# The last batch's queries turned by two DMA transposes instead of sixteen TensorE transposes, with the list of steps remade

## The chip, the cores and the metric

The kernel runs on one core of one Trainium2 chip. A core has five engines that run beside each other: TensorE (PE: matmuls, and transposes done as matmuls against an identity), VectorE (DVE), ScalarE (ACT), GpSimd (POOL) and SyncE (SP, which here only issues DMAs), and sixteen DMA engines that move data between HBM and the core's SBUF. The metric is device time in microseconds (us), the median over several executions. A profile of one further execution records every instruction; its span, from the first to the last instruction, is a little shorter than the time of the same execution.

## The reference

Efficient attention over 8 batches of 8 heads, 576 tokens and 64 elements a head, followed by a highway layer of width 512 over the 4608 tokens.

```
q_s = softmax(q, axis=-1)            # over the 64 elements of a head
k_s = softmax(k, axis=2)             # over the 576 tokens
kv  = einsum('bhsd,bhse->bhde', k_s, v)
x   = einsum('bhsd,bhde->bhse', q_s, kv)   # heads side by side: 4608 x 512
H   = maximum(x @ w_h, 0)
T   = sigmoid(x @ w_t + b_t)
out = T * H + (1 - T) * x            # float32, 4608 x 512
```

All inputs and the output are float32; the kernel works in fp16 inside.

## The kernel before

**Tiles.** The 4608 rows are worked in 36 tiles of 128 rows. Two batches make nine tiles: four of the even batch, four of the odd one, and one that holds half of each. Tiles 27 to 30 belong to batch 6, tiles 31 to 34 to batch 7, and tile 35 to both. Tiles 0, 4 and 5 are worked in two halves.

**Steps of a batch.** `k`, `v` and `q` (L180, L192) load it, 1152 KB of each. In batches 4 to 7 (`WIDE`, L186) a row of the landed query is one whole token with all its heads: two loads of 512 KB (L198) bring the tokens of the four whole tiles, and a third of 128 KB (L202) those of the shared tile. `ek` (L249) and `eq` (L293) are exponentials on ACT; `vc` (L255) casts V to fp16 on POOL, ACT or DVE, two calls a batch; `kv` (L261) multiplies K and V in 72 small matmuls; `kr`, `kn` (L277, L282) normalise the product on DVE. `qt` (L307) turns the exponential of the query on PE, so that the head's elements lie on the partitions: groups 0 and 1 are eight 128x128 transposes each for two tiles, group 2 is two transposes for the shared tile. The result is in PSUM, and `qc` (L326) copies it to SBUF on DVE or ACT.

**Steps of a tile.** `xu` (L337) multiplies the turned query, which it asks of `turned_q` (L334), by the batch's KV: four matmuls, whose last columns are the softmax's sums. `rs` and `x` (L356, L361) divide by them on DVE. `xt` (L368) turns x in four PE transposes, `xe` (L375) copies that to SBUF on DVE or ACT. `bw` (L382) puts the bias in PSUM, on PE, or on ACT if its step is marked `:A`; `mt` and `mh` (L394, L402) are the two products of four 512-wide matmuls each; `th` (L416) is a tanh on ACT. `dd` (L425), `uu` (L435), `ee` (L429) and `oo` (L451) combine them: in most tiles `dd` and `uu` run on DVE and `oo` on POOL; in a tile whose `uu` is marked `:P` ("lifted", L411), `uu`, `ee` and `oo` all run on POOL. `st` (L462) stores, from SP or, marked `:A`, from ACT's queue.

**What sets the order.** `ORDER` (L16 to L62) is a list of steps written out in advance; a step names its function, its batch or tile and a part, and after a colon an engine. The program is recorded in that order, so every engine executes its own steps in the order of the list and waits where an input or a buffer is not ready. Loads and nearly all stores go through SP's one queue: an SP instruction that waits holds up those behind it. `fill` (L165) steps are matmuls on zeros whose result nobody reads.

**Buffers.** The pools at L86 to L101 rotate: three landing tiles for each of k, q and v, four turned-query tiles, three each for `dd`, `uu`, `ee` and `th`, seven pairs of output tiles, two PSUM banks each for the two products, one for turned queries.

Of the kernel before, what the change touches and what calls it, by code (L numbers as in the profile page):

```python
# [9 lines left out]
FP16 = mybir.dt.float16  # L10
# [3 lines left out]


ORDER = """  # L16
b_0 b_32 k_0_1 v_0_1 k_0_3 setuppool k_0_0 setupdve vc_0_1 fill_16 q_0_0 ek_0_0 ek_0_3 v_0_2 eq_0_0 v_0_0 ek_0_1 fill_16
fill_12 vc_0_2:A bsplit k_0_2 vc_0_0:A v_0_3 q_0_4 vc_0_3:D fill_6 ek_0_2 bp eq_0_1 w_h_0 qt_0_0 fill_4 w_h_2 w_t_0
whd_1:P kv_0_0 whd_3:P fill_9 qc_0_0 kv_0_1 kr_0_0 fill_12 w_t_2 qt_0_1 fill_2 bc kr_0_1 kn_0_1 kn_0_0 xu_1_0 whd_0
rs_1_0 qc_0_1:A x_1_0 whd_2:P xu_0_1 rs_0_1 fill_12 fill_2 x_0_1 xu_0_0 whc_2 eq_0_2 xu_3_0 q_1_0 whc_0:A fill_9 rs_3_0  # L20
xt_1_0 wtc_2:P k_1_2 v_1_2 eq_1_0 wtc_0:P bw_1 qt_0_2 x_3_0 rs_0_0 xe_1_0:D ek_1_2 xt_3_0 xe_3_0:D xu_2_0 rs_2_0 x_0_0
vc_1_3 x_2_0 bw_3 mh_1_0 mh_3_0 xt_0_0 xt_0_1 xe_0_0 mt_3_0 mt_1_0 dd_1 ek_1_3 qc_0_2 v_1_0 th_3_0 qt_1_0 vc_1_2:A
xe_0_1:D mh_0_1 th_1_0 dd_3 k_1_0 uu_3_0 q_1_4 uu_1_0 q_2_0 kv_1_1 kr_1_1 qc_1_0:A xt_2_0 mh_0_0 xe_2_0 kn_1_1 bw_2
vc_1_0 bw_0 mt_0_1 dd_0 xu_5_1 ek_1_1 ek_1_0 mt_2_0 xu_4_1 rs_5_1 x_5_1 rs_4_1 vc_1_1 kv_1_0 x_4_1 eq_1_1 mt_0_0 xt_5_1
kr_1_0 th_2_0 eq_1_2 qt_1_1 k_2_0 xe_5_1 bw_5 kn_1_0 qc_1_1 v_2_0 xu_5_0 th_0_0 mt_5_1 rs_5_0 q_3_0 k_3_0 x_5_0 qt_1_2
ee_0 xu_4_0 bw_4 xt_5_0 xe_5_0:D xu_6_0 rs_4_0 rs_6_0 mh_2_0 x_4_0 xt_4_1 oo_1_0 uu_0_0:P xt_4_0 x_6_0 qc_1_2:A oo_0_0
mt_5_0 xu_8_0 eq_2_2 dd_2 mh_5_0 eq_2_0 fill_0 mh_5_1 xe_4_0:D xe_4_1 rs_8_0 eq_2_1 x_8_0 xt_6_0 dd_5 th_5_0 qt_2_0
xu_7_0 ek_2_2 oo_3_0 uu_2_0:P ee_2 mt_4_1 xe_6_0:D mt_4_0 qc_2_0 rs_7_0 ek_2_0 x_7_0 v_3_0 mh_4_1 vc_2_0:A xt_8_0 mh_4_0
uu_5_0 mh_6_0 qt_2_1 vc_2_2 xe_8_0:D kv_2_0 bw_6:A dd_4 th_4_0 mh_8_0 dd_6 q_4_0 kr_2_0 uu_4_0:P oo_2_0 kn_2_0 bw_8:A
qc_2_1:A eq_3_0 mt_6_0 xu_9_0 xt_7_0 dd_8 rs_9_0 mt_8_0 qt_2_2 x_9_0 xu_10_0 th_6_0 xe_7_0 k_4_0 xt_9_0 uu_6_0 oo_5_0  # L30
mh_7_0 th_8_0 rs_10_0 q_4_9 bw_7:A qc_2_2 x_10_0 ee_4 qt_3_0 xu_12_0 xe_9_0 oo_4_0 eq_3_2 uu_8_0 mt_7_0 oo_6_0 vc_3_0
ek_3_0 rs_12_0 bw_10:A th_7_0 eq_3_1 xt_10_0 mh_9_0 dd_7 x_12_0 vc_3_2 xe_10_0:D xu_11_0 qc_3_0 v_4_0 oo_8_0 xt_12_0
rs_11_0 x_11_0 uu_7_0 mh_10_0 xe_12_0:D mt_10_0 ek_3_2 v_5_0 bw_9 kv_3_0 k_5_0 q_5_0 th_10_0 bw_12:A eq_4_0 dd_10 mt_9_0
dd_9 uu_10_0:P kr_3_0 th_9_0 xt_11_0 qt_3_1 st_1_1:A kn_3_0 xu_14_0 mt_12_0 xe_11_0:D rs_14_0 mh_12_0 x_14_0 ee_10
uu_9_0 oo_7_0 xu_13_0 xt_14_0 dd_12 eq_4_1 oo_10_0 mh_11_0 oo_9_0 th_12_0 rs_13_0 xe_14_0:D bw_11:A v_6_0 qc_3_1:A
x_13_0 mt_11_0 uu_12_0 xu_15_0 ek_4_0 xt_13_0 bw_14:A mh_14_0 rs_15_0 xe_13_0 x_15_0 dd_11 qt_3_2 xu_16_0 oo_12_0
mt_14_0 ek_4_2 xt_15_0 qc_3_2 th_11_0 rs_16_0 th_14_0 vc_4_2 ee_11 dd_14 bw_13:A vc_4_0:A x_16_0 st_1_0 mh_13_0
xe_15_0:D uu_11_0:P xu_17_0 uu_14_0 rs_17_0 x_17_0 vc_5_2 bw_16:A xt_16_0 qt_4_0 xe_16_0 dd_13 qc_4_0 mt_13_0 kv_4_0
kr_4_0 qt_4_1 th_13_0 eq_4_2 oo_11_0 kn_4_0 xt_17_0 mh_15_0 q_5_9 qc_4_1 bw_15:A xu_18_0 k_6_0 mt_16_0 ek_5_2 qt_4_2
vc_5_0 rs_18_0 ek_5_0 st_3_0 ee_13 eq_5_1 dd_15 uu_13_0:P eq_5_0 ee_15 th_16_0 bw_17:A x_18_0 mh_16_0 oo_14_0 kv_5_0  # L40
xe_17_0:D dd_16 xt_18_0 qc_4_2 mt_15_0 th_15_0 ee_16 qt_5_1 kr_5_0 kn_5_0 oo_13_0 xe_18_0:D xu_20_0 qc_5_1 bw_18:A
rs_20_0 q_6_0 q_7_0 mh_17_0 mt_17_0 x_20_0 vc_6_2:A uu_15_0:P th_17_0 xu_21_0 qt_5_0 st_3_1 dd_17 rs_21_0 x_21_0 mt_18_0
xt_21_0 mh_18_0 oo_15_0 qc_5_0 vc_6_0:A xe_21_0:D xt_20_0 uu_16_0:P st_5_0 eq_5_2 oo_16_0 xu_19_0 st_5_1 th_18_0 uu_17_0
rs_19_0 xe_20_0:D bw_20:A mh_21_0 bw_21:A x_19_0 mt_20_0 xu_22_0 dd_21 dd_18 ek_6_2 ee_18 st_7_1 uu_18_0:P oo_17_0
rs_22_0 xt_19_0 ek_6_0 x_22_0 xe_19_0:D mt_21_0 mh_20_0 th_21_0 st_7_0 k_7_0 th_20_0 bw_22:A kv_6_0 xt_22_0 dd_20 qt_5_2
uu_21_0 eq_6_1 bw_19:A mh_19_0 kr_6_0 xe_22_0:D eq_6_0 kn_6_0 v_7_0 uu_20_0:P ee_20 st_10_1 mt_22_0 oo_18_0 dd_19
oo_20_0 q_7_9 xu_23_0 rs_23_0 qc_5_2 mh_22_0 x_23_0 th_22_0 qt_6_0 oo_21_0 xt_23_0 xu_24_0 mt_19_0 dd_22 eq_7_1 xe_23_0
mh_23_0 rs_24_0 qc_6_0 eq_7_0 bw_23:A x_24_0 xu_25_0 rs_25_0 xt_24_0 ee_22 x_25_0 th_19_0 qt_7_0 xe_24_0:D qc_7_0:A
uu_19_0 st_14_1 oo_19_0 mt_23_0 xu_26_0 rs_26_0 th_23_0 xt_25_0 qt_6_1 x_26_0 mh_24_0 bw_24:A xu_27_0 dd_23 uu_22_0:P
xe_25_0 mt_24_0 oo_22_0 qc_6_1:A ek_7_0 rs_27_0 xt_26_0 st_10_0 xe_26_0 x_27_0 th_24_0 qt_7_1 xu_29_0 uu_23_0 dd_24  # L50
rs_29_0 st_8_0 mh_25_0 x_29_0 bw_25:A oo_23_0 ek_7_2 vc_7_2 mh_26_0 uu_24_0 bw_26:A xu_28_0 rs_28_0 xt_29_0 xe_29_0
mt_25_0 q_6_9 th_25_0 x_28_0 qc_7_1:A dd_25 st_16_1:A vc_7_0 dd_26 oo_24_0 uu_25_0 mt_26_0 xt_27_0 th_26_0 bw_27:A
kv_7_0 bw_29:A xe_27_0:D mh_29_0 uu_26_0:P kr_7_0 mh_27_0 xt_28_0 st_12_1:A st_12_0 st_16_0:A kn_7_0 dd_29 xu_31_0
eq_6_2 mt_27_0 rs_31_0 x_31_0 ee_26 oo_25_0 xe_28_0 st_14_0 dd_27 mt_29_0 oo_26_0 xu_30_0 rs_30_0 xt_31_0 qt_6_2 th_27_0
mh_28_0 bw_28:A mt_28_0 th_29_0 xe_31_0:D x_30_0 st_21_0 uu_27_0:P st_19_0 xu_33_0 uu_29_0 eq_7_2 mh_31_0 xt_30_0 qc_6_2
rs_33_0 st_17_0:A bw_31:A th_28_0 xe_30_0 st_26_0 x_33_0 qt_7_2 dd_28 ee_27 dd_31 mt_31_0 st_25_0 oo_27_0 xu_32_0
oo_29_0 uu_28_0 xt_33_0 th_31_0 mh_30_0 xe_33_0 rs_32_0 x_32_0 st_23_0 bw_33:A mh_33_0 xu_34_0 uu_31_0 dd_33 mt_33_0
rs_34_0 xt_32_0 qc_7_2 bw_30:A x_34_0 xe_32_0:D dd_30 mt_30_0 xu_35_0 xt_34_0 th_33_0 oo_28_0 bw_32:A rs_35_0 th_30_0
uu_30_0 xe_34_0 bw_34:A mh_32_0 x_35_0 dd_32 ee_33 mt_32_0 oo_31_0 mt_34_0 st_31_0 xt_35_0 uu_33_0:P oo_33_0 mh_34_0
th_32_0 uu_32_0 st_28_0 oo_30_0 bw_35_1 xe_35_0 mt_35_1 st_33_0 th_34_0 dd_34 bw_35_0:A th_35_1 st_30_0 uu_34_0 oo_32_0  # L60
oo_34_0 mh_35_0 st_32_0:A mt_35_0 st_34_0 dd_35 uu_35_1 th_35_0 uu_35_0 oo_35_0 oo_35_1:D st_35_1:A st_35_0
# [4 lines left out]
def kernel(  # L66
# [10 lines left out]
    nc = tc.nc  # L77
    B, H, S, D = q.shape
    DM = H * D
    P = 128  # L80
    NP = 64
# [9 lines left out]
    eqp = pool("eqp", 4)  # L91
# [25 lines left out]
    T = {}  # L117

    def once(name, make):
        if name not in T:  # L120
            T[name] = make()
        return T[name]
# [57 lines left out]
    def load_kv(which):  # L180
        def step(e, b, c):
            n = (1, 2)[b] if b < 2 else 4
            nc.sync.dma_start(landing(which, b)[:, c:c + n], rows_of(which, b)[:, c:c + n])  # L183
        return step

    WIDE = (4, 5, 6, 7)  # L186
    MAIN = 4 * 2 * 4 * D
# [274 lines left out]
    def st(e, i, h):  # L462
# [60 lines left out]
```

## Time and profile before

| | us |
|---|---|
| time, median of 3 runs (lowest, highest) | 122.44 (122.19, 122.52) |
| time of the profiled execution | 122.46 |
| its span | 120.6 |
| PE busy | 110.4 (92%), of it 100 fills 13.4 |
| DVE busy | 94.0 (78%) |
| ACT busy | 95.1 (79%) |
| POOL busy | 88.5 (73%), 90 instructions |
| PE transposes of a query, 8 in a group (L316) | start to start 0.45 for the eight |
| ACT copy of a turned group (L330) | 1.01 to 1.04 |

The profile's timeline gives an instruction's start and its length; the start of the next one on the same engine tells how fast they really follow each other, which is less than the length where instructions overlap in a pipeline. A bracket behind a row tells how long the engine was idle before it and what ended the wait. The granted TensorE clock is full (0.998).

The DMA engines moved 40.08 MB in the span, a mean of 332 GB/s.

### The profile page before, as it was taken

Reading aid. Unit: us, or ns where it says so; the run is one execution under the profiler, and the core shown is the slowest. Engines: PE = TensorE matmul, PEld = TensorE weight load, DVE = VectorE, ACT = ScalarE, POOL = GpSimd, SP = SyncE. Lnnn points to the kernel's source line nnn. Section 1 sums busy time; section 2 is a strip of 40 time slices with the busy share of each in tenths; the row PEclk is TensorE's granted clock in tenths of the full one; section 3 lists DMA queues with packets and bytes.
Section 4 is the critical chain, followed back from the end, with each engine's and each line's share of the span. In section 5 each row is a group of like instructions: output and inputs, shape, how many; then the busy total and the mean of one; then the engine's idle time right before and its main releaser. Section 6 shows DMA issues by size and latency. Waiting matters only on the chain.

```text
span 120.6 us, 3576 instructions
## 1 busy us (share of the span) xinstructions
PE 110.4 (92%) x1426; PEld 69.2 (57%) x1426; DVE 94.0 (78%) x226; ACT 95.1 (79%) x146; POOL 88.5 (73%) x90
## 2 busy tenths in 40 slices
PE   5984999989899999999999999999999999999920
PEld 4863897454555656565657565556566655654510
DVE  5600877589599889989998998989789988999570
ACT  4049565798859999899999899999999966758710
POOL 5300043356597499999899999799999799969960
PEclk9999999999999999999999999999999999999999
DMA  3999999999999999999999999999999989910865
GB/s 105 296 359 387 382 379 377 391 374 387 390 386 393 391 387 358 379 361 394 396 373 365 380 389 355 358 377 376 382 366 293 280 201 353 353 42 23 325 261 174
DMA packets 22628, 40.08 MB, mean 332 GB/s; under 512 B 3282, under 2 KB 9682, under 8 KB 22612
## 3 DMA queue, kind: packets, MB, share of 16 engines
q1 hardware_dynamic: 21856, 38.15, 89.1%
q10 hardware_dynamic: 756, 1.71, 4.7%
q8 instruction: 11, 0.18, 0.6%
q14 instruction: 5, 0.04, 0.1%
HBM read 30.41 MB, written 9.44 MB: 331 GB/s over the span
## 4 chain that ended last, share of the span: by engine, by line
PE 60%; DMA 17%; ACT 9%; SPq 6%; issue 2%; DVE 2%; POOLq 1%; DVEq 0%; ACTq 0%
PE tps L399 21%; PE gps L407 20%; DMA q<-in_q_dram 17%; SPq L183 6%; PE turned L372 6%; PE xu L350 5%; PE qps L316 3%; PE kv L268 3%; ACT qe L297 2%; ACT ek L252 2%; PE qps L321 1%; ACT tps L423 1%; ACT tps L387 1%; ACT v L258 1%; ACT th L421 1%
## 5 line engine op out<-in xcount | busy, mean ns | idle before, releaser
L399 PE MATMUL tps<-w16t,xT 128*128 128x512 f16 (+1 forms) x148 | 36.8, 373 | 0.1
L407 PE MATMUL gps<-w16h,xT 128*128 128x512 f16 x144 | 36.5, 379 | 0.0
L365 DVE TENSOR_TENSOR x<-xu,rs 128x512 f16<-128x512 f32 (+1 forms) x39 | 25.0, 646 | 1.7
L460 POOL TENSOR_TENSOR o<-u,x 128x512 f32<-128x512 f16 (+1 forms) x22 | 24.9, 1136 | 1.7 <-DVE u L442 1.3
L427 DVE SCALAR_TENSOR_TENSOR d<-x,gps 128x512 f16<-128x512 f16 x36 | 24.0, 679 | 1.5 <-PE gps L407 1.1
L252 ACT ACTIVATE ek<-k 128x1152 f16<-128x1152 f32 (+1 forms) x20 | 18.9, 971 | 5.2 <-DMA k<-in_k_dram 5.2
L399 PEld LDWEIGHTS <-xT 128*128 128x128 f16 x148 | 13.4, 98 | 11.6 <-DVE xT L379 0.5
L440 POOL TENSOR_TENSOR u<-th,d 128x512 f16<-128x512 f16 x14 | 16.2, 1156 | 4.2 <-DVE rz L280 2.5
L407 PEld LDWEIGHTS <-xT 128*128 128x128 f16 x144 | 12.8, 98 | 10.6 <-ACT xT L379 0.3
L387 ACT COPY tps<-ball 128x512 f32<-128x512 f32 (+1 forms) x29 | 16.8, 586 | 2.1 <-DVE u L442 1.9
L433 POOL TENSOR_TENSOR e<-d,x 128x512 f16<-128x512 f16 x14 | 16.2, 1155 | 2.7 <-DVE d L427 2.7
L258 POOL CAST v<-v 128x1152 f16<-128x1152 f32 (+1 forms) x12 | 12.2, 1029 | 6.2 <-DMA v<-in_v_dram 6.2
L460 POOL TENSOR_TENSOR o<-u,e 128x512 f32<-128x512 f16 x14 | 16.1, 1155 | 0.5
L442 DVE SCALAR_TENSOR_TENSOR u<-tps,d 128x512 f16<-128x512 f32 (+1 forms) x23 | 15.1, 661 | 1.7 <-ACT tps L423 1.5
L167 PE MATMUL turned<-blank 128*128 128x256 f16 x100 | 13.4, 292 | 1.3 <-POOL blank L149 1.3
L350 PE MATMUL xu<-kvb,eq 128*128 128x130 f16 (+1 forms) x160 | 14.6, 224 | 0.0
L372 PE MATMUL turned<-idh,x 128*128 128x128 f16 x144 | 14.1, 219 | 0.4 <-ACT xT L379 0.3
L423 ACT ACTIVATE tps<-tps 128x512 f32<-128x512 f32 (+1 forms) x23 | 13.0, 566 | 1.7 <-PE tps L399 1.7
L350 PEld LDWEIGHTS <-eq 128*128 128x128 f16 (+1 forms) x160 | 10.5, 100 | 5.9 <-DVE x L365 1.5
L372 PEld LDWEIGHTS <-x 128*128 128x128 f16 x144 | 10.1, 98 | 5.1 <-issue 0.7
L297 ACT ACTIVATE qe<-q 128x1024 f16<-128x1024 f32 (+1 forms) x12 | 10.0, 843 | 3.9 <-DMA q<-in_q_dram 3.9
L167 PEld LDWEIGHTS <-blank 128*128 128x128 f16 x100 | 10.1, 105 | 3.0 <-POOL blank L149 1.3
(49 smaller groups left out, 127.7 us busy)
## 6 DMA issues: line engine op xcount, KB each, us to landing
k<-in_k_dram SPq DMA_DIRECT2D x6, 1152.0 KB, 12.8
v<-in_v_dram SPq DMA_DIRECT2D x6, 1152.0 KB, 12.4
q<-in_q_dram SPq DMA_DIRECT2D x10, 512.0 KB, 12.2
out_dram<-o SPq DMA_DIRECT2D x17, 256.0 KB, 5.6
out_dram<-o SPq DMA_DIRECT2D x6, 512.0 KB, 3.9
q<-in_q_dram SPq DMA_DIRECT2D x2, 1152.0 KB, 15.5
out_dram<-o ACTq DMA_DIRECT2D x6, 256.0 KB, 2.6
q<-in_q_dram SPq DMA_DIRECT2D x2, 640.0 KB, 10.3
```

Source lines behind the costliest of these rows:

```text
L167: nc.tensor.matmul(spare, blank[:, 0:P], blank[:, 0:2 * P], start=True, stop=True, skip_group_check=True)
L252: nc.scalar.activation(t[:, :, c:c + n].rearrange("p j c d -> p c j d"), T[f"k32{b}"][:, c:c + n].rearrange("p c (j d) -> p c j d", j=NJ), ...
L350: nc.tensor.matmul(dst, turned_q(b, jp, n), kvb[b % NKV][:, hh, kk], start=True, stop=True, skip_group_check=True)
L365: nc.vector.tensor_mul(t[:, k0:k1], sums(i, k)[:, :, :, 0:64], T[f"rs{i}_{k}"][:, 0:k1 - k0].unsqueeze(3).to_broadcast([P, k1 - k0, 4, D]))
L372: nc.tensor.matmul(t[:, n], T[f"x{i}"][:, n * P:(n + 1) * P], idh, is_transpose=True, start=True, stop=True, skip_group_check=True)
L387: nc.scalar.copy(t[:, cs], ball[:, cs])
L399: nc.tensor.matmul(T[gate(i, k)][:, cs], T[f"xT{i}"][:, n], w16["t"][:, n, cs], start=False, stop=(n == parts[-1] and not first), skip_gro ...
L407: nc.tensor.matmul(t, T[f"xT{i}"][:, n], w16["h"][:, n], start=(first and n == parts[0]), stop=(n == parts[-1] and not (first and len(part ...
L427: nc.vector.scalar_tensor_tensor(t, T[f"x{i}"], -0.5, T[f"gps{i}"], op0=ALU.mult, op1=ALU.max)
L433: eng.tensor_add(T[f"e{i}"], T[f"d{i}"], T[f"x{i}"])
L440: eng.tensor_mul(t, T[f"th{i}"], T[f"d{i}"])
L460: eng.tensor_add(t[:, cs], T[f"u{i}"][:, cs], T[f"{'e' if lifted(i) else 'x'}{i}"][:, cs])
```

## The change

The sixteen PE transposes of batch 7's two groups (`qt_7_0`, `qt_7_1`) and their two copies (`qc_7_0`, `qc_7_1`, both on ACT) are gone. In their place a new step `dt` issues, from SP, one DMA transpose for each group: it reads 128 rows of 1024 fp16 elements (256 KB) from the exponential in SBUF and writes eight turned 128x128 blocks to a new tile `eqd` in SBUF. `turned_q` takes batch 7's whole tiles from there. Group 2 of batch 7, and all other batches, are turned on PE as before.

```diff
+    def dt(e, b, g):
+        t = once(f"eqd{b}", lambda: eqp.tile([P, 4, 2, 2, NP * 2], FP16, tag="eqd", bufs=1, name=f"eqd_{b}"))
+        eng = nc.scalar if e == "A" else nc.sync
+        main = T[f"qe{b}"].rearrange("p j c d -> p (j c d)")[:, MAIN // 2 * g:MAIN // 2 * (g + 1)]
+        eng.dma_start(t[:, 2 * g:2 * g + 2].rearrange("p j h k t -> p (j h k) t"), main, transpose=True)
+
     def turned_q(b, jp, n):
+        if f"eqd{b}" in T and jp < 4:
+            return T[f"eqd{b}"][:, jp, n % 2, n // 2]
         return T[f"eq{b}_{jp // 2}"][:, jp % 2, n]
```

The whole list of steps is new. Its first lines, the lines with batch 7's query and KV, and its end:

```diff
 ORDER = """
-b_0 b_32 k_0_1 v_0_1 k_0_3 setuppool k_0_0 setupdve vc_0_1 fill_16 q_0_0 ek_0_0 ek_0_3 v_0_2 eq_0_0 v_0_0 ek_0_1 fill_16
-fill_12 vc_0_2:A bsplit k_0_2 vc_0_0:A v_0_3 q_0_4 vc_0_3:D fill_6 ek_0_2 bp eq_0_1 w_h_0 qt_0_0 fill_4 w_h_2 w_t_0
+b_0 b_32 k_0_0 k_0_1 k_0_3 q_0_0 setuppool k_0_2 ek_0_0 ek_0_1 v_0_3 ek_0_2 v_0_1 setupdve v_0_0 bsplit fill_12 fill_12
+fill_9 eq_0_0 fill_16 fill_16 qt_0_0 vc_0_0:A q_0_4 v_0_2 eq_0_1 vc_0_1:D fill_12 w_t_0 vc_0_3 w_t_2 qc_0_0 kv_0_0
...
-rs_22_0 xt_19_0 ek_6_0 x_22_0 xe_19_0:D mt_21_0 mh_20_0 th_21_0 st_7_0 k_7_0 th_20_0 bw_22:A kv_6_0 xt_22_0 dd_20 qt_5_2
...
-mh_23_0 rs_24_0 qc_6_0 eq_7_0 bw_23:A x_24_0 xu_25_0 rs_25_0 xt_24_0 ee_22 x_25_0 th_19_0 qt_7_0 xe_24_0:D qc_7_0:A
...
-xe_25_0 mt_24_0 oo_22_0 qc_6_1:A ek_7_0 rs_27_0 xt_26_0 st_10_0 xe_26_0 x_27_0 th_24_0 qt_7_1 xu_29_0 uu_23_0 dd_24
...
-mt_25_0 q_6_9 th_25_0 x_28_0 qc_7_1:A dd_25 st_16_1:A vc_7_0 dd_26 oo_24_0 uu_25_0 mt_26_0 xt_27_0 th_26_0 bw_27:A
-kv_7_0 bw_29:A xe_27_0:D mh_29_0 uu_26_0:P kr_7_0 mh_27_0 xt_28_0 st_12_1:A st_12_0 st_16_0:A kn_7_0 dd_29 xu_31_0
...
+xe_23_0 k_7_0 th_22_0 mt_23_0 xt_24_0 uu_22_0 mh_23_0 rs_25_0 eq_6_2 x_25_0 eq_7_1 th_23_0 eq_7_0 xe_24_0:D xu_26_0
+uu_19_0:P bw_24:A mh_24_0 dd_23 st_10_0:A st_10_1 ee_19 rs_26_0 xt_25_0 uu_23_0 mt_24_0 xe_25_0 dt_7_0 oo_19_0 x_26_0
+xu_27_0 qc_6_1 th_24_0 st_14_0 dd_24 bw_25:A oo_22_0 mh_25_0 ee_24 rs_27_0 xt_26_0 mt_25_0 bw_26:A vc_7_2:A x_27_0
+xu_29_0 xe_26_0:D oo_23_0 xt_27_0 vc_7_0 qt_6_2 th_25_0 q_7_9 ek_7_2 dd_25 dt_7_1 rs_29_0 mt_26_0 ek_7_0 x_29_0 uu_25_0
+xu_28_0 mh_26_0 bw_27:A st_17_0 xe_27_0:D mh_27_0 st_14_1 uu_24_0:P rs_28_0 x_28_0 qc_6_2 st_12_0 oo_24_0 xt_29_0
+st_12_1 th_26_0 kv_7_0 oo_25_0 dd_27 st_23_0 dd_26 uu_26_0:P kr_7_0 mt_27_0 xe_29_0 bw_29:A xt_28_0 mt_29_0 th_27_0
+st_16_1 kn_7_0 xu_31_0 ee_26 mh_29_0 xe_28_0 st_25_0 rs_31_0 uu_27_0 x_31_0 oo_26_0 th_29_0 bw_28:A eq_7_2 dd_29 mh_28_0
+uu_29_0:P ee_29 xu_30_0 oo_27_0 rs_30_0 xt_31_0 x_30_0 xe_31_0 mt_28_0 st_26_0 th_28_0 bw_31:A dd_28 qt_7_2 bw_30:A
+st_8_0:A xt_30_0 xe_30_0:D xu_33_0 rs_33_0 mh_31_0 x_33_0 mt_31_0 dd_31 xt_33_0 th_31_0 xe_33_0 xu_32_0 rs_32_0 mt_30_0
...
-th_32_0 uu_32_0 st_28_0 oo_30_0 bw_35_1 xe_35_0 mt_35_1 st_33_0 th_34_0 dd_34 bw_35_0:A th_35_1 st_30_0 uu_34_0 oo_32_0
-oo_34_0 mh_35_0 st_32_0:A mt_35_0 st_34_0 dd_35 uu_35_1 th_35_0 uu_35_0 oo_35_0 oo_35_1:D st_35_1:A st_35_0
+xe_34_0 xt_35_0 bw_34:A dd_32 st_21_0 xe_35_0:D oo_33_0 th_32_0 st_16_0 oo_30_0 mh_34_0 st_19_0 uu_32_0 mt_34_0 st_28_0
+st_31_0 oo_32_0 bw_35_1 mh_35_0 st_33_0 fill_0 dd_34 th_34_0 mt_35_1 bw_35_0:A mt_35_0 uu_34_0 dd_35 th_35_1 th_35_0
+uu_35_1 st_30_0 fill_16 st_32_0 uu_35_0 oo_34_0 st_34_0 oo_35_0:D st_35_0 oo_35_1:D st_35_1:A
 """
```

Counted over the two lists: fills 100 before and 109 after; `bw` on PE 8 and 6, on ACT 29 and 31; lifted tiles 14 and 17, and `uu` on DVE 23 and 20; `xe` on ACT 17 and 20, on DVE 22 and 19; `qc` on ACT 8 and 5, on DVE 16 and 17; casts of `w_t` on POOL 2 and 1, on ACT none and 1; subtractions of the identity (`whd`) on POOL 3 and 4; `oo` on POOL 36 and 35. The weights `w_t` are loaded ahead of `w_h` instead of behind. Batches 0 and 1 and the weights are still loaded first, up to the last part of batch 1's query (`q_1_4`), then `q_2`, `k_2`, `v_2`; of the last batch `v_7` is now loaded ahead of `k_7`.

## The prediction

> **What bounds the kernel now.** I read the page's forty slices first (3.0 us each), to see who is full where.
>
> ```profile
> PE   5984999989899999999999999999999999999920
> POOL 5300043356597499999899999799999799969960
> DMA  3999999999999999999999999999999989910865
> ```
>
> PE is full almost to its end, but its first seven digits are partly `fill`. POOL is nearly as full from the middle on, and the DMA engines are full up to slice 32. So three things are close to binding, and each stage has to be looked at. Next I read the timelines of the opening, and the waits' last releasers.
>
> ```profile
> 20.55 1.89 PE L407 MATMUL gps<-w16h,xT 128*128 128x512 f16 x8
> ...
> 29.32 1.06 ACT L297 ACTIVATE qe<-q 128x1024 f16<-128x1024 f32 x1 [0.51 <-DMA q<-in_q_dram]
> ...
> 30.43 0.62 PE L321 MATMUL qps<-idh,qe 128*128 128x128 f16 x8 [0.44 <-ACT qe L297]
> ...
> 38.43 1.15 POOL L258 CAST v<-v 128x1152 f16<-128x1152 f32 x1 [0.70 <-DMA v<-in_v_dram]
> ```
>
> Up to 30.4 us the loads set the pace: `q_1_4` lands at 29.3, its exponential ends at 30.3, and `qt_1_1` starts on PE at 30.43. `v_2` lands at 38.4, and `kv_2` starts at 40.14. From there PE hardly stops: what its starts lose to 115.45 comes to some 2.5 us in small pieces, half of it around `kv`'s small matmuls, the longest 0.42. The chain of waits says the same: from 44.68 on it is PE alone, until the last matmul. These are two of its lines and its end:
>
> ```profile
> 50.74 0.21 PE tps L389
> ...
> 82.98 0.45 PE qps L316 x8
> ...
> 115.00 0.45 PE tps L399 x4
> 115.45 0.02 issue
> 115.48 0.38 ACT tps L423
> ```
>
> The bound is PE's work from 30.43 on, and then a tail of 5.1 us (120.6 - 115.45).
>
> **The opening.** Both lists load the same bytes ahead of `q_1_4`, so I take 29.3 for its landing again. The other half of the argument is whether PE has done as much by then. Before, it has done `mt` 0 to 3, `mh` 0, 1, 3, both halves of `kv_0` and `kv_1`, and the two halves of `xu` that need `qt_1_0`. In the new list, `w_t` comes where `w_h` came (15.2 and 16.6), so `mt_3` can start near 19.0, ahead of 20.55; `w_h` comes where `w_t` came (18.3 and 20.0), POOL subtracts the identity until 21.4 and ACT's two `whc` (1.0 each) end at 23.3, so `mh` is 2.8 us later than before. Both fit in front of `qt_1_1`: the same steps are done by 30.4, and one more half of `xu` (0.12). What hides the later `mh` is the wait for `q_1_4`; beyond 30.4 it would cost one for one. Then `kv_2` could start at 39.4 by the sum of PE's steps and waits for `v_2` to about 40.1, as before.
>
> **PE's sum from `qt_1_1`.** By the start-to-start times of the rows (0.86 for each `mt` or `mh`, 0.23 for `xu`, 0.22 for `xt`, 0.21 for `bw`, 0.45 for eight `qt`):
> - `qt_7_0` and `qt_7_1`: 2 x 0.45 = -0.90.
> - `bw_4` and `bw_9` go to ACT: 2 x 0.21 = -0.42.
> - the half `xu` done earlier: -0.12.
>
> -1.44 in all. The stage from 84 to 95 us where the transposes stood is one in which PE is full, so they were on the path. With the old stalls and pieces kept (0.8 of them the wait for `v_2`) PE ends at 115.45 - 1.44 = 114.0.
>
> **ACT and DVE.** Over the list ACT loses three `qc` of 0.9 and gains two `bw` (0.52), three `xe` (0.5) and one cast of 1.0: +0.8, most of it before 40 us. From `kv_2` on, ACT has 66 us of work and DVE 68 beside PE's 73.4. Their changes are taken at nothing; PE's work covers them.
>
> **POOL.** This one isn't free. Three more lifted tiles are six operations of 1.115 (start to start): +6.7; one `w_t` cast and half an `oo` go: -1.7; `whd` +0.4. From `kv_2` on I count 66 operations, 73.6 us, where before it was 70.9. POOL is free from `vc_2_2`'s end, 38.4 + 1.15 = 39.6. Run without a pause it ends at 113.2. Before, it had 6.6 us of gaps between 41 and 117, the longest 1.66 for `u<-th,d`. A fuller queue waits less; of the ten or so short gaps of 0.08 where an `oo` follows its own `ee` I keep 1.0, and for late inputs 1.2. The last full `oo` (tile 34) then ends at 115.4.
>
> **The tail.** Before, POOL was late here too:
>
> ```profile
> 115.29 1.15 POOL L460 TENSOR_TENSOR o<-u,x 128x512 f32<-128x512 f16 x1 [0.61 <-DVE u L442]
> ...
> 116.83 0.72 POOL L460 TENSOR_TENSOR o<-u,x 128x256 f32<-128x256 f16 x1 [0.39 <-POOL o L460]
> 117.06 0.37 ACTq L468 DMA_DIRECT2D out_dram<-o  x1
> 117.58 0.36 SPq L468 DMA_DIRECT2D out_dram<-o  x1
> ```
>
> From the last store's issue to the end is 3.0 us. The new list puts both last `oo` on DVE (0.4 each). By PE alone: 114.0, tanh to 114.4, `uu` 0.4, two `oo` 0.8, last issue at 115.6, end 118.6. But `st_34` stands ahead of `st_35_0` on SP and waits for POOL: 115.4 + 0.03 + its issue of 0.54, then 3.0 gives 119.0. The later one counts: **119.0**. The sixteen fills after the last matmul (16 x 0.11) feed nobody and end before the stores land.
>
> **The two DMA transposes.** `dt` waits on SP for `eq_7_1` and `eq_7_0`, about 87.5 by ACT's sum. Queued behind it on SP are `st_14_0`, `q_7_9`, `dt_7_1`, then stores; none is needed soon (`q_7_9` by `qt_7_2`, 101). In front of it in the DMA queue is `k_7`, near 91.1 (the last big load of before, issued at 79.8 with 10.9 to its landing, plus `q_6_9`), and a store of 0.7: it moves from about 91.8. It is needed by `xu_31`, near 97.9, the second by `xu_33`, near 101.5; behind a waiting `xu_31` all of PE stands.
>
> The trace has no DMA transpose. The nearest row is a plain transfer of the same size in the same quiet part:
>
> ```profile
> out_dram<-o ACTq DMA_DIRECT2D x6, 256.0 KB, 2.6
> ```
>
> With 2.6 each `dt_7_0` lands at 94.4 and `dt_7_1`, behind a store and `q_7_9` (1.1), at 98.1: 3.5 and 3.4 us spare. The Trainium skill speaks against this change: "VectorE: DVE Perf Modes", section "The three transpose paths", puts one 128x128 transpose at 390 ns on TensorE and 1309 ns by DMA. On PE the trace disagrees: eight in 0.45, 56 ns each, so PE's gain is 0.9 and not 6.2. If the 1309 held for eight blocks in turn, one `dt` took 10.5 us; `dt_7_0` would land at 102.3 and `dt_7_1` at 113.9, 12.4 after `xu_33` wants it. The same skill's "DMA: Bandwidth & Descriptors", section "Latency and other measured facts", gives a transpose 261 GB/s: 1.0 us for 262 KB, so an estimate of about the row. The ends are 1.0 and 10.5 us; I take 2.6[...]. A cost below nothing is excluded for `dt` itself.
>
> **Forecast.** 119.0 + 1.9 (the profiled execution's 122.46 against its span of 120.6) = **120.9 us**, 1.5 below that execution, and as much below the median of 122.44. Its own range is 119.9 to 121.7.
>
> **Rivals.**
> - *The transposes are late* (slower). Place: PE's wait of `xu_33` for `dt_7_1`. For it: [...]no row. Against it: idle DMA engines after 95. It decides from 2d + 1.1 = 9.7, d = 4.3 us each, and the gain is gone at about d = 5; at d = 7 the end is 5.4 later: 126.3, at 10.5 near 133. Chance 0.16.
> - *POOL paces the second half* (slower). With the 6.6 us of gaps of before, `oo_34` ends at 119.8, and the time is 119.8 + 3.6 + 1.9 = 125.3. It decides from 3.8 us of gaps. For it: POOL's slices of nines; against it: gaps shrink when a queue has a backlog. Chance 0.12.
> - *New waits eat part of it*: a remade list puts 0.4 to 0.9 us of PE gaps elsewhere (buffers of three, a late cast for a `kv`): 121.3 to 121.9. Chance 0.13, faster still.
> - *Hidden anyway*: `k_7` now comes last; `ek_7` is two exponentials of 1.1 after 91.1, so `kv_7` can't start before 93.5, where PE's sum gives 95. If the landing is 2 to 3 us later, no change, 122.4. Chance 0.09.
>
> The forecast keeps 0.50. Faster is 0.50 + 0.13 = 0.63, same 0.09, slower 0.16 + 0.12 = 0.28; 0.3% (0.4 us) is what a measurement of this kernel can tell from no change. The range goes from 119.8 (POOL without late inputs, PE alone) to 124.6, into the slow rivals, and leaves about 0.18 out.
>
> **What would show it.** Right: the first eight `qps` transposes of batch 1's second half start at 30.4 again; PE's last matmul at 114.0; `xu_31` and `xu_33` wait for no DMA; POOL's last full `oo` ends by 115.5; busy POOL near 94. Wrong: `qt_1_1` later than 31; PE's weight loads of `eqd` waiting for a DMA; gaps of PE ahead of a `kv` for a V cast; or SP's issue of a `dt` so long that stores bunch up at the end.

## The result, and the profile after

| | before | after |
|---|---|---|
| time, median (lowest, highest; runs) | 122.52 us (122.00, 123.40; 22) | 122.17 us (121.47, 122.48; 22) |
| profiled execution, its span | 122.46, 120.6 | 122.15, 120.4 |
| busy: PE, DVE | 110.4, 94.0 | 112.2 (109 fills in it), 91.9 |
| busy: ACT, POOL | 95.1, 88.5 | 95.6, 92.8 |

The ratio is 0.9956 [0.9938, 0.9975]. The change is faster, by 0.35 us where 1.5 were forecast, and the forecast's own range (119.9 to 121.7) doesn't hold it. The changed kernel measured again gave 0.9982 [0.9949, 1.0014]; this interval includes 1, so that run alone wouldn't tell the change from no change.

PE's slices of the changed kernel, 3.0 us each, and the shares of the chain of waits, first before, then after:

```profile
PE   5999698799999999999999999999999999999990
...
PE 60%; DMA 17%; ACT 9%; SPq 6%; issue 2%; DVE 2%; POOLq 1%; DVEq 0%; ACTq 0%
...
PE 40%; ACT 22%; DMA 16%; SPq 8%; DVE 8%; issue 3%; DVEq 0%
```

The digits of PE look as full as before. The chain tells more: PE's share of it was 60% and is 40%, ACT's has gone from 9% to 22% and DVE's from 2% to 8%. A slice of "9" says that PE is busy 90% of the time or more; it doesn't say that PE sets the pace.

**The opening** came later than before by 0.6. Two rows of its timeline (start, length, engine, line, operation, and in the bracket the idle time ahead of it):

```profile
29.93 1.36 ACT L297 ACTIVATE qe<-q 128x1024 f16<-128x1024 f32 x2 [0.20 <-DMA q<-in_q_dram]
...
31.07 0.61 PE L321 MATMUL qps<-idh,qe 128*128 128x128 f16 x8
```

`q_1_4` lands at 29.90, 0.6 later than before, and `qt_1_1` begins at 31.07 instead of 30.43.

**The stage of the transposes.** First the transposes themselves, by the rows of their tile (weight loads, the two issues with their shortest, median and longest time in ns, who waited for the tile, and the time from issue to landing):

```profile
L358 PEld LDWEIGHTS <-eqd x16: 97/98/101, 98.9 to 107.4; 128*128 128x128 f16 x16
...
L338 SPq DMA_TRANSPOSE eqd<-qe x2: 1404/1818/2232, 88.6 to 91.3; - x2
...
DMA to landing us min/median/max: 4.6/5.0/5.3
```

They landed at 93.90 and 95.91, and PE first read the tile at 98.9: nobody waited for them. What PE waited for stands in the waits of 84 to 97 us (who waited, for whom: us in total, times, longest). Before, it was little, and DVE waited for PE:

```profile
DVE rs L359 <- PE xu L350: 1.1, 3, 0.6
...
PEld L350 <- DVE x L365: 0.4, 2, 0.2
```

After:

```profile
PEld L358 <- DVE x L373: 1.9, 4, 0.8
DVE u L450 <- ACT qe L305: 1.0, 1, 1.0
```

Weight loads run ahead of the matmuls, so not all of the 1.9 need be lost. The loss is read from PE's starts: the time from each matmul's start to the next, less what that shape takes without a wait. From the first matmul of `kv_6` to the first of `kv_7` this rest was 0.23 before and is 1.00 after. The chain goes through other engines there:

```profile
85.23 0.59 ACT tps L431
85.82 0.33 ACT qe L305
86.15 0.13 issue
86.28 0.69 DVE u L450
86.97 0.12 DVE rs L367
87.10 0.02 issue
87.12 0.53 DVE x L373
```

and it stays on DVE until 94.1, where it had been PE alone. Read it so: `x_25` at 87.12 stands behind a `u` (`u_22`) that waited, and behind `x_25` stands PE's next `xu`, because there is one PSUM buffer for `xu` (in the expectations: the `xu` bank) and `x` empties it. The `qe` in the chain is only the last thing that ended ahead of the `u`. What `u_22` needs from ACT is its tanh (`tps` L431), which ended at 85.82, and DVE's wait for that is over at 85.86; for the 0.42 us from there to 86.28 the trace shows no reason.

**The end.** PE's last matmul of a product starts at 115.30; before, it was 115.17, and the forecast had PE end at 114.0. Behind it:

```profile
115.05 0.68 DVE L435 SCALAR_TENSOR_TENSOR d<-x,gps 128x512 f16<-128x512 f16 x1
115.21 1.15 POOL L468 TENSOR_TENSOR o<-u,x 128x512 f32<-128x512 f16 x1 [0.66 <-DVE u L450]
...
115.86 0.76 DVE L450 SCALAR_TENSOR_TENSOR u<-tps,d 128x256 f16<-128x256 f32 x2
116.64 0.76 DVE L468 TENSOR_TENSOR o<-u,x 128x256 f32<-128x256 f16 x2
117.10 0.46 SPq L476 DMA_DIRECT2D out_dram<-o  x1
117.44 0.37 ACTq L476 DMA_DIRECT2D out_dram<-o  x1
```

The end is now DVE's chain: `u_34`, `d_35`, two `u`, two `o`. From the start of that last matmul to the end it took 5.07 us, before 5.41.

**Where the 1.44 of PE's work went.** From the start of `qt_1_1` to the start of PE's last matmul of a product it is 84.73 us before and 84.23 after. By the times that its shapes take without a wait, PE's work in this part fell by 1.44, as forecast; so the rest, its waits, grew by 0.94, from 2.41 to 3.35. By stretch, before and after: `qt_1_1` to `kv_3` 1.35 and 1.12; `kv_3` to `kv_4` 0.23 and 0.68; `kv_4` to `kv_6` 0.44 and 0.27; `kv_6` to `kv_7` 0.23 and 1.00; from there 0.16 and 0.28. With the opening 0.64 later and the end 0.34 shorter, -1.44 + 0.94 + 0.64 - 0.34 gives -0.20, which is the difference of the two spans. The work did leave PE, and waits took its place.

### The profile page after: what moved, and what is told of

Its sections match the earlier page's. It is cut to its first block, busy times and chain, and to the rows that moved or that the text cites. A ratio compares the mean times of both kernels' runs of the same rounds, so it can differ in the third digit from the quotient of the medians.

```text
span 120.4 us, 3570 instructions
## 1 busy us (share of the span) xinstructions
PE 112.2 (93%) x1417; PEld 69.3 (58%) x1417; DVE 91.9 (76%) x221; ACT 95.6 (79%) x149; POOL 92.8 (77%) x95
## 4 chain that ended last, share of the span: by engine, by line
PE 40%; ACT 22%; DMA 16%; SPq 8%; DVE 8%; issue 3%; DVEq 0%
PE gps L415 14%; PE tps L407 14%; DMA q<-in_q_dram 9%; SPq L183 7%; DMA v<-in_v_dram 7%; ACT qe L297 5%; PE xu L358 4%; PE turned L380 4%; ACT ek L252 4%; ACT tps L431 3%; ACT tps L395 3%; PE kv L268 2%; DVE u L450 2%; ACT th L429 2%; DVE d L435 2%
## 5 line engine op out<-in xcount | busy, mean ns | idle before, releaser
L441 POOL TENSOR_TENSOR e<-d,x 128x512 f16<-128x512 f16 x17 | 19.6, 1161 | 3.1 <-DVE d L435 3.1
L468 POOL TENSOR_TENSOR o<-u,x 128x512 f32<-128x512 f16 x18 | 20.8, 1160 | 0.9 <-DVE u L450 0.9
L468 POOL TENSOR_TENSOR o<-u,e 128x512 f32<-128x512 f16 x17 | 19.6, 1160 | 0.7
L448 POOL TENSOR_TENSOR u<-th,d 128x512 f16<-128x512 f16 x17 | 19.7, 1161 | 0.4 <-POOL v L258 0.3
L167 PE MATMUL turned<-blank 128*128 128x256 f16 x109 | 14.8, 299 | 1.3 <-POOL blank L149 1.3
L450 DVE SCALAR_TENSOR_TENSOR u<-tps,d 128x512 f16<-128x512 f32 (+1 forms) x20 | 13.1, 657 | 2.7 <-ACT tps L431 1.2
L387 ACT COPY xT<-turned 128x512 f16<-128x512 f16 (+1 forms) x20 | 11.2, 562 | 4.3 <-PE turned L380 4.3
L431 ACT ACTIVATE tps<-tps 128x512 f32<-128x512 f32 (+1 forms) x20 | 11.2, 560 | 3.8 <-PE tps L407 3.8
L358 PEld LDWEIGHTS <-eq 128*128 128x128 f16 (+1 forms) x144 | 8.9, 101 | 8.2 <-DVE x L373 4.2
L167 PEld LDWEIGHTS <-blank 128*128 128x128 f16 x109 | 11.5, 107 | 3.5 <-POOL blank L149 1.3
```

The source lines that it names most:

```text
L167: nc.tensor.matmul(spare, blank[:, 0:P], blank[:, 0:2 * P], start=True, stop=True, skip_group_check=True)
L358: nc.tensor.matmul(dst, turned_q(b, jp, n), kvb[b % NKV][:, hh, kk], start=True, stop=True, skip_group_check=True)
L441: eng.tensor_add(T[f"e{i}"], T[f"d{i}"], T[f"x{i}"])
L448: eng.tensor_mul(t, T[f"th{i}"], T[f"d{i}"])
L468: eng.tensor_add(t[:, cs], T[f"u{i}"][:, cs], T[f"{'e' if lifted(i) else 'x'}{i}"][:, cs])
```

## Experiments

Single times scatter by some 0.8 us either way, most of it ahead of `qt_1_1`: with before's opening, instruction for instruction the same, it began between 29.56 and 31.23 in fourteen profiles. The loads make this scatter: in the thirteen profiles that tell when `q_1_4` landed, `qt_1_1` began 1.13 or 1.14 us later. Behind it the stretch from `qt_1_1` to `kv_3` and the two of the table repeat to a few hundredths (one kernel gave 16.15 and 16.02); the one from `kv_3` to `kv_6` does not, it took 27.93 to 28.34. So beside the ratio I give the stretch from the first matmul of `kv_6` to the first of `kv_7`, in which batch 7's query was turned, and the one from there to the start of PE's last matmul of a product. In the remade list other work lies in these stretches, so they are compared only within one list. Each ratio is to the runs of before on the same chip in the same session (their medians were 122.39 to 122.82). A row rests on 6 to 12 runs of its kernel, the first of the change on 22.

| kernel | median us | ratio, 95% | kv_6 to kv_7 | kv_7 to last product |
|---|---|---|---|---|
| before | | 1 | 16.51 | 19.72 |
| transposes alone, in before's list | 122.15 | 0.9977 [0.9942, 1.0013] | 16.26 | 19.72 |
| transposes left out | 122.40 | 0.9978 [0.9947, 1.0009] | 16.27 | 19.72 |
| turned twice | 121.99 | 0.9961 [0.9930, 0.9992] | 16.50 | 19.72 |
| fills put back | 123.14 | 1.0064 [1.0035, 1.0094] | 17.46 | 19.72 |
| four biases on PE | 124.39 | 1.0138 [1.0099, 1.0176] | 18.12 | 19.72 |
| two copies on ACT | 122.64 | 1.0006 [0.9970, 1.0042] | 16.03 | 20.59 |
| one copy on ACT | 122.09 | 0.9959 [0.9928, 0.9989] | 16.02 | 19.72 |
| three steps moved | 122.68 | 1.0013 [0.9984, 1.0042] | 16.28 | 20.18 |
| steps moved and one copy | 122.51 | 1.0006 [0.9985, 1.0028] | 16.27 | 20.18 |
| one copy and two biases | 121.52 | 0.9896 [0.9856, 0.9937] | 16.15 | 19.72 |
| the same again | 122.03 | 0.9918 [0.9887, 0.9949] | 16.02 | 19.72 |
| and the remade end | 121.73 | 0.9915 [0.9882, 0.9949] | 16.02 | 19.72 |
| two biases alone, no transposes | 122.32 | 0.9960 [0.9937, 0.9984] | 16.50 | 19.72 |
| the change | 122.17 | 0.9956 [0.9938, 0.9975] | 18.11 | 18.86 |
| the change again | 122.14 | 0.9982 [0.9949, 1.0014] | 18.16 | 18.86 |
| remade list, turned on PE | 124.09 | 1.0124 [1.0076, 1.0172] | 20.05 | 18.98 |
| remade list, old opening | 122.11 | 0.9972 [0.9931, 1.0014] | 17.76 | 18.86 |
| remade list, `u_22` moved | 121.78 | 0.9917 [0.9892, 0.9942] | 17.76 | 18.86 |
| and one copy on ACT | 122.91 | 1.0014 [0.9988, 1.0041] | 18.96 | 18.86 |

### The two halves of the change

> The changed kernel once more, to see which parts of its trace repeat. Theory A (the remade list loses in the opening, in new waits of PE and in the tail what it gains in PE work): batch 1's second group of transposes again starts near 31.0 us, 0.6 later than in the kernel before, and PE again waits some 0.9 us more after kv_2 than in the kernel before; time near 122.2. Theory B (the later opening was chance of one execution): the group starts at 30.4 in this trace, and the span is 0.6 shorter than 120.4.

Both parts of its trace repeat, as theory A has it: `qt_1_1` began at 30.96, and PE's waits from `kv_6` to `kv_7` came to 1.05.

> The list of the kernel before with nothing changed but batch 7's two groups: each pair of PE transposes and copy becomes one DMA transpose at the place of the PE transposes. Theory A (the transposes' 0.9 us of PE is a true gain and the list spoils it): 0.7 to 1.0 us under the kernel before, near 121.6; xu_31 and xu_33 wait for no DMA. Rival B (PE's time in this stage is covered, and the tail or DVE's x sets the end): within 0.3 us of the kernel before. Rival C (the transposes delay something): slower.

The transposes alone, in before's list:

```diff
-... th_19_0 qt_7_0 xe_24_0:D qc_7_0:A ...
+... th_19_0 dt_7_0 xe_24_0:D ...
-... th_24_0 qt_7_1 xu_29_0 ...
+... th_24_0 dt_7_1 xu_29_0 ...
-... x_28_0 qc_7_1:A dd_25 ...
+... x_28_0 dd_25 ...
```

> The remade list with batch 7's two groups turned on PE and copied by ACT again, at the nearest places where the one PSUM bank for turned queries is free. Theory A: the list by itself is 0.3 to 0.7 us slower than the kernel before, 122.9 to 123.2, and about 0.9 above the changed kernel. Rival B (the list makes the gain and the transposes none): as fast as the changed kernel, 122.2.

The remade list alone, with batch 7 turned on PE at these places:

```diff
+... qc_6_1 qt_7_0 ...   dd_24 qc_7_0:A ...
+... st_12_0 qt_7_1 ...   th_26_0 qc_7_1:A ...
```

The whole times alone decide little. The transposes alone came out within 0.3 us of before, as rival B has it, and their interval includes 1. The kernel below that turns twice keeps all of before's work on PE and yet measured 0.9961; so the 0.25 is read from the stretch, not from the medians. The remade list turned on PE was slower than both of its forecasts.

The DMA transposes by themselves bring 0.25 of the 0.90 us that leave PE (16.51 to 16.26). In the remade list the same exchange is worth 1.9 (20.05 to 18.11), 124.09 against 122.14 for the whole. I chose the places of the old steps there, so this isn't what the list with the best places would take; it does show that the worth of the transposes is a matter of the list and not a number that can be added. In the profile of the transposes alone, PE's waits from 84 to 97 us are these:

```profile
PEld L359 <- DVE x L374: 1.4, 4, 0.5
DVE rs L368 <- PE xu L359: 0.8, 2, 0.6
```

and DVE's timeline shows no bracket between 86.31 and 97:

```profile
86.00 0.21 DVE L368 RECIPROCAL rs<-xu 128x8 f32<-128x8 f32 x1 [0.60 <-PE xu L359]
86.31 0.69 DVE L374 TENSOR_TENSOR x<-xu,rs 128x512 f16<-128x512 f32 x1
86.92 0.41 DVE L388 COPY xT<-turned 128x512 f16<-128x512 f16 x1
87.25 0.68 DVE L451 SCALAR_TENSOR_TENSOR u<-tps,d 128x512 f16<-128x512 f32 x1
```

Before, DVE waited 1.1 us for PE's `xu` in this window, in three pieces. Two of them, 0.21 and 0.60, end ahead of the first transposes (85.91). This is the only one behind them:

```profile
89.65 0.21 DVE L359 RECIPROCAL rs<-xu 128x8 f32<-128x8 f32 x1 [0.27 <-PE xu L350]
```

With the transposes off PE it is gone, the other two are left, and from 86.31 on PE waits for DVE. So 0.27 is about what the transposes could bring here, and 0.25 came: DVE was the next wall, that close behind PE.

### The opening

> The changed kernel with all steps ahead of batch 1's second query group taken from the list of the kernel before, in that list's order (loads too, and tiles 1 and 3 not lifted), and the rest in the remade order. Theory A: the group starts at 30.4 again, and the whole is 0.4 to 0.7 us under the changed kernel, near 121.6. Rival B (the later stage catches up whatever the opening does, because loads or POOL pace it): the same time as the changed kernel.

```diff
-(the remade list's steps ahead of qt_1_1)
+(before's steps ahead of qt_1_1; what is left over follows in the remade order)
```

No gain, but the run is inconclusive: the list joined out of two halves made waits of its own, of 0.79 at 31.4 and 0.52 at 33.8, `qt_1_1` began at 32.29, and its profiled execution was a long one (123.11). The opening's 0.6 therefore rests on profiles: `qt_1_1` began at a median of 30.4 in the fourteen with before's opening, and of 31.0 in the five with the remade one (30.80 to 31.62). The two ranges overlap.

Two things come together in the remade opening. `q_1_4` landed late: at 29.66 to 30.43 in four of the five, at 28.42 to 30.09 with before's opening. And PE was not done with its earlier steps. In the fifth profile, that of the table's last kernel, the query landed at 29.36, its exponential ended at 30.64, and yet:

```profile
29.58 1.37 ACT L298 ACTIVATE qe<-q 128x1024 f16<-128x1024 f32 x2
...
31.04 0.61 PE L322 MATMUL qps<-idh,qe 128*128 128x128 f16 x8
```

There is no bracket behind PE's row: PE came straight from other steps. In all five the first `mh` started at 22.95 to 23.62, where before it was 20.55. How much the order of the weights' loads makes of this and how much the order of the first steps stays open.

### Was it the DMA, PE, ScalarE or VectorE?

> The list of before with qt_7_0, qt_7_1, qc_7_0 and qc_7_1 taken out and no DMA in their place; the whole tiles of batch 7 (31 to 34) read the turned query of batch 6, so their output is another one. This is the ceiling of what taking the sixteen transposes and two copies away can bring in this list. Theory C (the stage 84 to 97 us was balanced: once PE is 0.9 shorter, VectorE, which works without a pause from 86.3 to 97, and ScalarE set the pace): as the transposes alone in before's list, 122.0 to 122.3, a ratio of 0.997 to 0.999 to before. Rival D (the DMA transposes themselves cost what was missing, through SP's 1.4 to 3.1 us of issue, or the traffic of 512 KB): 121.4 to 121.7, a ratio of 0.991 to 0.994.

```diff
-... qt_7_0 ... qc_7_0:A ... qt_7_1 ... qc_7_1:A ...
     def turned_q(b, jp, n):
+        if b == 7 and jp < 4:
+            b = 6
```

16.27, as with the DMA transposes (16.26): in this stretch they cost nothing. The whole came out 0.1 above what the first theory gave and 0.7 above the rival's range.

> The transposes alone in before's list, with the sixteen transposes done on PE as well, as before, into a bank that nothing reads; only their two copies by ScalarE stay out. So PE has before's load and ScalarE 2.05 us less. Theory F and C (before was paced by PE itself there, with 0.14 us of waits): 16.45 to 16.55 from kv_6 to kv_7, the time of before, 122.3 to 122.6. Rival (the 0.25 us that the transposes bring comes from ScalarE's relief, not PE's): 16.2 to 16.3, 122.1.

```diff
+... dt_7_0 qt_7_0 ...
+... dt_7_1 qt_7_1 ...
```

With the sixteen transposes back on PE the stretch is 16.50 again, before's to 0.01, though ACT has its two copies less. PE's waits are before's as well:

```profile
PEld L359 <- DVE x L374: 0.4, 2, 0.2
```

So ACT's relief brought nothing; PE did pace before, with little room. The whole was lower than expected, 121.99 where 122.3 to 122.6 was; its profiled execution, 121.71, has an early opening, 29.61, so the opening may be the reason; for the other runs there is no profile.

> The transposes alone in before's list, with four matmuls of filling (0.86 us in all on PE) put back behind the two dt, so that PE has its old load there and ScalarE keeps its relief of 2.05 us. Theory C (PE has slack there now, since VectorE sets the pace): no more than 0.25 above the transposes alone, 122.1 to 122.5. Rival (PE still paces the stage): 0.7 to 0.9 above, 122.9 to 123.1.

```diff
+... dt_7_0 fill_4 ...
+... dt_7_1 fill_4 ...
```

0.99 above the transposes alone, near the rival's 0.7 to 0.9 (the stretch 1.20); but the edit brought a wait of its own. A fill writes the bank `turned` and stood still until that was copied:

```profile
91.34 0.60 PE L168 MATMUL turned<-blank 128*128 128x256 f16 x4 [0.82 <-ACT xT L388]
```

It decides nothing; turning twice is the clean form of the same question.

> The transposes alone in before's list, with bw of tiles 24 to 27 as matmuls on PE (+0.84 us of PE) instead of copies on ScalarE (-2.1 us of ScalarE). If ScalarE's biases and the two tps banks pace the stage: 0.3 to 0.5 faster than the transposes alone, 121.7. If VectorE paces it: within 0.2 of it, 122.0 to 122.3. If PE paces it: 0.6 to 0.8 slower, 122.8.

```diff
-bw_24:A bw_25:A bw_26:A bw_27:A
+bw_24 bw_25 bw_26 bw_27
```

The stretch is 1.9 longer, more than any of the three forecasts; PE's own work is 0.84 of it, and this wait the rest. A bias waits for a bank that a `u` empties; on ACT the wait held up what ACT had behind it, on PE it holds up what PE has:

```profile
PE tps L398 <- DVE u L451: 1.0, 2, 0.7
```

> The transposes alone in before's list, with the copies xe of tiles 24 and 27 on ScalarE, which is idle at 86.3 (0.76 us) since qc_7_0 is gone, instead of on VectorE (-0.41 us each there). Theory C (VectorE sets the pace from 86.3 to 97): kv_7 begins 0.3 to 0.7 earlier than 95.3 and the time is 121.5 to 121.9. Rival (ScalarE or PE paces): 122.1 to 122.4, no gain.

> The transposes alone in before's list, with the one copy xe_24 on ScalarE, in the place that qc_7_0 left free, and xe_27 left on VectorE. Measured by the stretch from the first matmul of kv_6 to that of kv_7, which comes out the same to 0.03 us from run to run: 16.50 in before, 16.26 with the transposes alone, 16.26 with them left out. Theory C (VectorE without a pause sets the pace): 15.9 to 16.05, and 0.2 to 0.35 off the whole, since nothing is lost behind kv_7. Theory F (the wait is the turn of the one xu bank: xu, rs, x, next xu take 1.5 to 1.6 us, and PE has only 1.31 us of other work between two xu where a group of transposes stood): 16.2 to 16.3, no gain by this edit.

```diff
-xe_24_0:D
+xe_24_0
-xe_27_0:D
+xe_27_0
```

(the second pair in the run with two copies alone). Taking `xe_24` from DVE, 0.41 us in length and 0.33 from start to start, gave 0.24 more in the stretch: 16.02. That is what the theory of VectorE expects and the theory of the `xu` buffer's turn denies. `xe_27` has no such room on ACT; there it stands behind two biases and comes late, so PE lost 0.87 behind `kv_7` and the whole gained nothing:

```profile
97.04 1.04 PE L416 MATMUL gps<-w16h,xT 128*128 128x512 f16 x4 [0.69 <-ACT xT L388]
```

> The transposes alone in before's list, and three steps moved so that PE has other work between two xu: qt_6_1 ahead of xu_26, mh_25 ahead of xu_29, xu_28 and rs_28 behind mt_25. No engine's sum changes. Theory F: the waits of PE from 84 to 97 us fall from 0.8 to 0.3 or less, kv_6 to kv_7 takes 15.7 to 15.85, the whole 121.6 to 121.75. Theory C (VectorE's sum sets the pace): 16.2 to 16.3 and 122.1, no gain.

> Both edits: the three steps moved and xe_24 on ScalarE. Theories C and F together (the xu bank's turn and VectorE are both near): 15.6 to 15.7 from kv_6 to kv_7 and 121.5 to 121.6 for the whole, the 0.9 us of the transposes recovered nearly in full. If something else sets the pace (ScalarE, or POOL, which is 98% busy from 84 to 99 us): 16.2 or more, 122.1.

```diff
-... mt_23_0 xu_26_0 ...   xt_25_0 qt_6_1 ...
+... mt_23_0 qt_6_1 xu_26_0 ...   xt_25_0 ...
-... xu_29_0 ... mh_25_0 ...
+... mh_25_0 xu_29_0 ...
-... xu_28_0 rs_28_0 ... mt_25_0 ...
+... mt_25_0 xu_28_0 rs_28_0 ...
```

Neither gained. Other work between two `xu` didn't shorten the stretch (16.28), and with `xu_28` moved back DVE stood idle for it 1.0 us, so that the copy `xT` of tile 27 behind it came later and PE lost 0.46 more after `kv_7`. With the copy moved as well, the 0.24 of that copy is lost again (16.27), and this is the range that the expectation gave to "something else", ScalarE or POOL. In that run DVE waited 2.1 us for PE's `xu` from 84 to 98, so in this list DVE's sum isn't the pace either; these three moves made a new wait in PE's order. That DVE was the next wall in before's own order rests on the one copy and on its timeline without a bracket. Whether POOL stands close behind it no run tested.

### The remade list's own wait

> The changed kernel with one step moved on VectorE: uu_22 behind rs_25 and x_25 instead of ahead of them. In the changed kernel VectorE stands idle 1.04 us ahead of that u, which waits for ScalarE, and rs_25 and x_25, whose sums were ready at 85.2, stand behind it; PE then waits 0.44 us at 87.2 for x_25. Theory C' (the remade list made this wait by VectorE's order): kv_6 to kv_7 falls from 18.11 to 17.65 or 17.75, the whole by 0.35 to 0.45 to 121.7 to 121.8. Rival (VectorE's sum paces to 97, the wait only moves to 93.7): 17.95 to 18.15, 122.1.

> As the run with u_22 moved, and xe_24 on ScalarE too, which has 0.48 and 0.34 us of idle time ahead of its work at 89.5 and 90.4. Theory C (VectorE is a second wall close behind): the remaining wait at 93.7 (0.28) goes as well, 17.4 to 17.55 from kv_6 to kv_7 and 121.45 to 121.6 for the whole. Rival (ScalarE has no room at this place): no better than the run with u_22 alone, or up to 0.3 worse.

```diff
-... xt_24_0 uu_22_0 mh_23_0 rs_25_0 eq_6_2 x_25_0 eq_7_1 ...
+... xt_24_0 mh_23_0 rs_25_0 eq_6_2 x_25_0 uu_22_0 eq_7_1 ...
```

With `u_22` behind `x_25` the 1.0 us of idle DVE is gone:

```profile
85.78 0.21 DVE L368 RECIPROCAL rs<-xu 128x8 f32<-128x8 f32 x1
86.09 0.69 DVE L374 TENSOR_TENSOR x<-xu,rs 128x512 f16<-128x512 f32 x1
86.70 0.68 DVE L451 SCALAR_TENSOR_TENSOR u<-tps,d 128x512 f16<-128x512 f32 x1
```

`x_25` now starts 0.75 after its `xu` where it took 2.3, the stretch falls by 0.35 to 17.76, and the whole to 0.9917. But the kernel with the old opening has 17.76 too, with `u_22` in its old place. There that `u` starts 0.08 us after its tanh has ended; in the changed kernel, in its repeat and in the remade list turned on PE it starts some 0.45 after it. So the 0.35 goes with this late start: it can be had by moving the step, but the step's place alone doesn't make it, and why the `u` starts late there the trace doesn't tell. It doesn't come from the transposes, since the list without them has it as well. With `xe_24` on ACT on top it gets worse: in this list ACT does it behind two exponentials, and PE stands.

```profile
89.53 1.04 PE L416 MATMUL gps<-w16h,xT 128*128 128x512 f16 x4 [1.21 <-ACT xT L388]
```

### The two other terms, each alone

> Before's list with the DMA transposes, xe_24 on ScalarE (the kernel of the run with one copy moved), and the biases bw_4 and bw_9 on ScalarE as the remade list has them. The prediction's term: PE 0.42 shorter and ScalarE free enough: 0.35 to 0.42 less from qt_1_1 to kv_3 or to kv_4, 121.6 to 121.75 for the whole. Rival (ScalarE's chain of tanh and biases paces the tiles from 30 to 57 us, as the chain of waits of the changed kernel has it): 0 to 0.15 less, 121.95 to 122.1.

> As the run with the biases, and its list ends with the remade list's steps behind xt_35. The prediction's term for the end was 0.5 us from PE's last product to the last store. Its own theory: 0.4 to 0.5 less behind the last product. Rival (VectorE's chain u_34, d_35, two u, two o, which the changed kernel shows there, sets the end): 0.1 to 0.35 less.

> The kernel with the DMA transposes in before's list, xe_24, bw_4 and bw_9 on ScalarE, once more. From its stretches (0.24 and 0.24 us less from kv_6 to kv_7, 0.29 less from qt_1_1 to kv_3): 0.7 to 0.8 below before, a ratio of 0.993 to 0.9945. If its first result (0.9896) was no chance: 0.988 to 0.991.

> Before's list with bw_4 and bw_9 on ScalarE and nothing else: the sixteen transposes stay on PE. If the terms add up: 0.3 below before, a ratio of 0.997 to 0.998, with 16.5 us from kv_6 to kv_7 and 0.29 less from qt_1_1 to kv_3. If the gain of the kernel with both came from the biases: 0.991 to 0.994.

```diff
-bw_4 ... bw_9
+bw_4:A ... bw_9:A
```

The two biases take 0.27 off the stretch from `qt_1_1` to `kv_3` (20.45 before, 20.17 to 20.18 in the four runs that have them), not 0.42: at 32 to 33 us PE stands 0.23 us for an `x` of DVE, where it didn't before. The remade end brings nothing by itself (5.28 to 5.24 us from the start of PE's last matmul of a product to the end, less than either theory gave). With the transposes, one copy and the biases together the sum is 0.25 + 0.24 + 0.27 = 0.76; the two measurements are 0.68 and 1.3 below before, so the first, larger gain wasn't confirmed. That kernel (0.9896, 0.9918) and the changed one with `u_22` moved (0.9917) have lower ratios than the change; only the first of these intervals lies wholly below the change's, and that one its repeat didn't give. That they are faster than the change is not shown.

## Why the prediction was wrong

The mechanisms that it names as rivals for the large losses didn't come: the first transpose landed 5.0 us before PE read it, the chain of waits has no POOL in it (2.3 us of gaps from 41 to 117), and `k_7` held up nobody. The direction was right, the size was not. Of its own signs of being wrong one came clearly: `qt_1_1` began at 31.07, later than 31.

- **The step that failed:** "With the old stalls and pieces kept", which rests on "Their changes are taken at nothing; PE's work covers them." The -1.44 of work came in full; the waits, put at no change, grew by 0.94. Where the transposes stood, PE was full and did set the pace (16.50 with the transposes on PE, though ACT had less to do), as the prediction says. But its sum counted the whole 0.90 as gain, without asking who is next. In before's list DVE stood 0.25 us behind: 0.25 of the 0.90 came, the other 0.65 turned into PE's waits for DVE's `x`, and one 0.41 us copy taken from DVE brought 0.24 more. The working compared sums from `kv_2` to the end; in the stage itself, from 84 to 99 us, DVE was busy for 13.06 of 15, in a ring in which the next `xu` needs the buffer that DVE's `x` empties.
- **New waits in the remade list:** named as a rival with 0.4 to 0.9 us and a chance of 0.13. It came: 0.35 with the late start of `u_22`, and 0.45 more from `kv_3` to `kv_4`, where the chain is on ACT up to 56.8. The cause of neither is shown.
- **The opening:** the second step that failed, "the same steps are done by 30.4". `qt_1_1` is later in all five profiles of that opening, by 0.6 at the median, and once PE came to it only at 31.04 though the query had landed by 29.36. The prediction had said itself that a later `mh` would cost one for one beyond 30.4.
- **The biases:** -0.42 was -0.27.
- **The end:** the sum counted 0.1 for it (5.1 to 5.0), since it had the last store wait for POOL; by PE alone it would have been 0.5. It was 0.34, more than was counted, and by another path: `oo_34` ended on POOL at 116.36 instead of 115.4, but the last stores waited for DVE, which must first do `u_34` and `d_35`. In before's list the same stretch took between 5.28 and 5.41 from run to run, and in the remade one between 5.06 and 5.13, so 0.15 to 0.35 is what can be said.
- **The landing of the transposes:** forecast at 94.4 and 98.1, measured at 93.90 and 95.91. `k_7`, which is ahead of them, landed at 91.70 (forecast 91.1). Nothing hung on it, since they were read from 99.1 on, a microsecond later than forecast.

## What to carry to other kernels

A saving on the engine that sets the pace is worth at most the distance to the next wall, and that distance is read in the stage itself. Look for the brackets of the second engine in which it waits for the first, and count only those behind the place of the saving: here DVE's one wait of 0.27 for PE, where 0.25 was gained. Where engines work in a ring with a single buffer, look for the next engine's chain before summing instructions. When a list is remade for one change, measure the change in the old list too, and set the work that left against the waits that came, stretch by stretch.

## What the runs showed of the hardware

A DMA transpose of 128 x 1024 fp16 from SBUF to SBUF (256 KB) landed 4.6 and 5.3 us after the start of its issue in the changed kernel, and 4.0 to 5.3 over all the runs whose profile tells it. That is not its own time: `k_7` and `q_7_9` were still landing beside it. Its issue held SP for 1.4 and 2.2 us there, and up to 3.7 in other runs, where the issue of a store in the same part of the kernel took SP some 0.5:

```profile
88.57 1.40 SPq L338 DMA_TRANSPOSE eqd<-qe  x1
90.08 0.53 SPq L488 DMA_DIRECT2D out_dram<-o  x1
```

For the stretch from `kv_6` to `kv_7` that was nothing (16.26 with them, 16.27 without).
